# Sliding-window attention before a SwiGLU block: each query block scored on the 128 keys up to its end, and another opening order

## The chip, the cores and the metric

One core of a Trainium2 chip. The metric is the device time of one execution in microseconds (us). The span in a profile, from the first to the last instruction, is some 2 us less. Engines: PE is TensorE (its weight loads are listed apart), DVE is VectorE, ACT is ScalarE, POOL is GpSimd; SP issues the DMAs. The granted clock is the share of full speed at which PE may run; in these traces it is 1.0 or 0.5 ("halved"). To turn is to transpose.

## The reference

```
q, k, v: (8 batches, 8 heads, 576 tokens, 64), float32
scores = q k^T / 8, kept where 0 <= i - j < 64; softmax; times v
x = (4608 tokens, 512)                      # the heads side by side
out = (silu(x w_gate) * (x w_val)) w_out    # 512 -> 1536 -> 512
```

## The kernel before

Tokens run through in 36 groups g of 128 (two query blocks of 64), in bf16. A group needs scores on its own 128 keys, and its first 64 queries also need the group before. Since 576 is 9 blocks of 64, in every ninth block a sequence starts, and nothing before it counts. The feed-forward works on tiles t of 512 tokens with 12 steps m; `gv` makes the two hidden products (in the PSUM buffers `g_ps` and `v_ps`) and the tanh, `finish` the two DVE operations `sg` and `hT`, one step later.

```
def scores(g, hs=(0, 1)):                  # two half calls a group
    ...
    for h in hs:
        for i in range(2):
            for a in range(2):             # two row tiles of 64: 128 queries on own keys
                matmul(ps[a][:, i, 0:P], tokens(kT, g, p, a), tokens(qT, g, p, a), tile_position=(64 * a, 0))
            if prev:                       # 64 queries on the keys of the group before
                for a in range(2): matmul(ps[a][:, i, P:n], tokens(kT, g - 1, p, a), ...)
        for a in range(2):
            act.activation(e, ps[a][:, :, 0:n], AF.Exp, scale=0.125)
            dve.tensor_mul(e, e, mk...)    # the mask, 128x384
...
def cast_v(n, eng, cs=(0, 1)): ...         # one cast of 128x512 a group, on POOL
...
loads(0); loads(1); weights_gv(0..2)       # the opening
warm(30)                                   # dummy matmuls
pack(0, "k_f", dve); pack(0, "q_f", act); turn_k(0); turn_q(0)   # turned on PE in fp32
scores(0); scores(1); ... turn_x(3)        # groups 0 to 3
for m in range(12): step(0, m) ...         # only then feed-forward of tile 0
...
for w in range(8, NG):                     # the steady loop, one group a round
    step(t, 3 * s);     scores(w + 6, (0,)); turn_x(w + 4)
    step(t, 3 * s + 1); scores(w + 6, (1,)); products(w + 5, (0,))
    step(t, 3 * s + 2); products(w + 5, (1,)); ...; project(t - 1, s)
```

The softmax here doesn't subtract the row's maximum and nothing guards it: scores larger than these inputs give would overflow.

## Time and profile before

| | before |
|---|---|
| time | 389.8 us (2 runs, 389.55 to 390.04) |
| span | 387.1 us |
| PE busy | 361.2 us, 93% |
| mean granted clock of PE | 0.960 |
| loop with attention, 22 rounds | 203.3 us (122.1 to 325.4) |

Of the groups of instructions, these three are what the change replaces (busy us, mean ns of one, then idle time ahead of them and what ended it):

```profile
L171 DVE TENSOR_TENSOR E<-E,mask 128x384 bf16<-128x384 bf16 (+1 forms) x144 | 54.1, 383 | 73.5 <-ACT E L170 71.1
...
L170 ACT ACTIVATE E<-s_ps 128x384 bf16<-128x384 f32 (+1 forms) x144 | 61.1, 477 | 24.9 <-PE s_ps L164 21.6
...
L140 POOL CAST vb<-v_f 128x512 bf16<-128x512 f32 x36 | 23.3, 653 | 11.0 <-DMA v_f<-in_v_dram 10.3
```

An idle time counts only on an engine that is the bound, and these three are not. They matter as neighbours of PE.

### The profile page before, as it was taken

Reading aid. Unit: us, or ns where it says so; the run is one execution under the profiler, and the core shown is the slowest. Engines: PE = TensorE matmul, PEld = TensorE weight load, DVE = VectorE, ACT = ScalarE, POOL = GpSimd, SP = SyncE. Lnnn points to the kernel's source line nnn. Section 1 sums busy time; section 2 is a strip of 40 time slices with the busy share of each in tenths; the row PEclk is TensorE's granted clock in tenths of the full one; section 3 lists DMA queues with packets and bytes.
Section 4 is the critical chain, followed back from the end, with each engine's and each line's share of the span. In section 5 each row is a group of like instructions: output and inputs, shape, how many; then the busy total and the mean of one; then the engine's idle time right before and its main releaser. Section 6 shows DMA issues by size and latency. Waiting matters only on the chain.

```text
span 387.1 us, 7051 instructions
## 1 busy us (share of the span) xinstructions
PE 361.2 (93%) x2674; PEld 189.0 (49%) x2718; DVE 247.2 (64%) x552; ACT 185.8 (48%) x358; POOL 65.0 (17%) x82
## 2 busy tenths in 40 slices
PE   8679988988878999999999999999999999999996
PEld 3443455855555444444444444444444444444442
DVE  3764797856665666667666666766666667654430
ACT  2464769635456554444544444454444554332321
POOL 4403142502142103030302022020302000000000
PEclk9756999999996999999999999999999999999999
DMA  9969999719539587696967667686828000000102
GB/s 205 300 195 242 323 323 217 156 39 180 152 73 187 127 122 152 144 168 120 164 142 145 134 141 143 131 150 124 163 62 180 32 30 27 30 27 27 56 33 103
DMA packets 130849, 52.89 MB, mean 137 GB/s; under 512 B 102144, under 2 KB 124672, under 8 KB 130816
## 3 DMA queue, kind: packets, MB, share of 16 engines
q1 hardware_dynamic: 130816, 52.44, 62.2%
q8 instruction: 21, 0.34, 0.4%
q14 instruction: 12, 0.10, 0.1%
HBM read 37.75 MB, written 9.44 MB: 122 GB/s over the span
## 4 chain that ended last, share of the span: by engine, by line
PE 83%; ACT 5%; DMA 4%; DVE 4%; issue 1%; SPq 1%; POOL 0%; POOLq 0%; ACTq 0%
PE o_ps L263 24%; PE g_ps L246 21%; PE v_ps L246 21%; PE s_ps L158 4%; PE ao_ps L186 3%; DMA k_f<-in_k_dram 3%; PE xtp L210 3%; ACT E L170 2%; PE w_ps L275 2%; PE tp L116 2%; DVE E L171 2%; PE ao_ps L191 2%; DMA v_f<-in_v_dram 2%; DVE x_b L197 1%; PE s_ps L164 1%
## 5 line engine op out<-in xcount | busy, mean ns | idle before, releaser
L246 PE MATMUL g_ps<-xT,wg 128*128 128x512 bf16 (+1 forms) x458 | 113.5, 364 | 4.8 <-DVE sg L257 2.8
L246 PE MATMUL v_ps<-xT,wv 128*128 128x512 bf16 (+1 forms) x469 | 113.3, 362 | 0.6
L171 DVE TENSOR_TENSOR E<-E,mask 128x384 bf16<-128x384 bf16 (+1 forms) x144 | 54.1, 383 | 73.5 <-ACT E L170 71.1
L263 PE MATMUL o_ps<-wo,hT 128*128 128x512 bf16 x421 | 96.7, 379 | 0.5
L257 DVE SCALAR_TENSOR_TENSOR sg<-th,g_ps 128x512 f32<-128x512 f32 (+1 forms) x120 | 75.2, 627 | 24.4 <-ACT th L251 24.3
L251 ACT ACTIVATE th<-g_ps 128x512 f32<-128x512 f32 (+1 forms) x120 | 66.7, 556 | 48.9 <-PE g_ps L246 45.7
L258 DVE TENSOR_TENSOR hT<-sg,v_ps 128x512 bf16<-128x512 f32 (+1 forms) x120 | 76.1, 634 | 9.2 <-DVE sg L257 0.5
L170 ACT ACTIVATE E<-s_ps 128x384 bf16<-128x384 f32 (+1 forms) x144 | 61.1, 477 | 24.9 <-PE s_ps L164 21.6
L246 PEld LDWEIGHTS <-wv 128*128 128x128 bf16 x480 | 47.7, 99 | 49.0 <-issue 2.7
L246 PEld LDWEIGHTS <-wg 128*128 128x128 bf16 x480 | 44.4, 99 | 39.9 <-issue 6.8
L263 PEld LDWEIGHTS <-hT 128*128 128x128 bf16 x432 | 40.7, 98 | 44.7
L158 PE MATMUL s_ps<-qT,kT 64*128 64x128 bf16 x288 | 25.5, 225 | 11.2 <-ACT E L170 5.6
L123 POOL CAST q_fb<-q_f 128x1024 bf16<-128x1024 f32 x10 | 10.4, 1040 | 136.4 <-DMA q_f<-in_q_dram 120.4
L197 DVE TENSOR_TENSOR x_b<-ao_ps,r 128x256 bf16<-128x256 f32 x72 | 30.6, 425 | 2.5
L186 PE MATMUL ao_ps<-vb,E 128*128 128x65 bf16 x288 | 27.4, 201 | 2.1 <-DVE x_b L197 1.6
L158 PEld LDWEIGHTS <-kT 64*128 64x128 bf16 x288 | 14.1, 96 | 28.7 <-issue 26.0
L186 PEld LDWEIGHTS <-E 128*128 128x128 bf16 x288 | 21.7, 102 | 8.9 <-DVE x_b L197 2.2
L211 ACT COPY xT<-xtp 128x512 bf16<-128x512 bf16 x36 | 21.3, 591 | 8.4 <-PE xtp L210 8.4
L140 POOL CAST vb<-v_f 128x512 bf16<-128x512 f32 x36 | 23.3, 653 | 11.0 <-DMA v_f<-in_v_dram 10.3
L191 PE MATMUL ao_ps<-vb,E 128*128 128x65 bf16 x256 | 25.1, 201 | 0.0
L191 PEld LDWEIGHTS <-E 128*128 128x128 bf16 x256 | 19.3, 102 | 3.3
L109 POOL CAST k_fw<-k_f 128x1024 bf16<-128x1024 f32 x7 | 9.6, 1370 | 66.0 <-DMA k_f<-in_k_dram 29.0
(72 smaller groups left out, 181.2 us busy)
## 6 DMA issues: line engine op xcount, KB each, us to landing
v_f<-in_v_dram SPq DMA_DIRECT2D x32, 256.0 KB, 5.9
k_f<-in_k_dram SPq DMA_DIRECT2D x20, 256.0 KB, 3.9
q_f<-in_q_dram SPq DMA_DIRECT2D x20, 256.0 KB, 4.2
w_f<-in_moe_w_gate_dram SPq DMA_DIRECT2D x6, 512.0 KB, 6.6
w_f<-in_moe_w_val_dram SPq DMA_DIRECT2D x6, 512.0 KB, 6.7
wo_f<-in_moe_w_out_dram SPq DMA_DIRECT2D x6, 512.0 KB, 6.5
k_f<-in_k_dram SPq DMA_DIRECT2D x5, 512.0 KB, 6.1
q_f<-in_q_dram SPq DMA_DIRECT2D x5, 512.0 KB, 6.1
```

The costliest lines, as they stand in the source:

```text
L140: eng.tensor_copy(vb[n % VR][:, c, :, 0:D], v_f[:, c])
L158: nc.tensor.matmul(ps[a][:, i, 0:P], tokens(kT, g, p, a), tokens(qT, g, p, a), tile_position=(64 * a, 0),)
L170: act.activation(e, ps[a][:, :, 0:n], AF.Exp, scale=0.125)
L171: dve.tensor_mul(e, e, mk[:, 0:n].unsqueeze(1).to_broadcast([P, 2, n]))
L186: nc.tensor.matmul(o_ps[:, i, :], E[:, y, 0:P], vb[g // 2 % VR][:, g % 2, y, :], start=True, stop=not prev,)
L191: nc.tensor.matmul(o_ps[:, i, :], E[:, y, P:2 * P], vb[(g - 1) // 2 % VR][:, (g - 1) % 2, y, :], start=False, stop=True,)
L197: dve.tensor_mul(x_b[:, 256 * h:256 * h + 256].rearrange("r (y d) -> r y d", y=4), o_ps[:, :, 0:D], r[:].unsqueeze(2).to_broadcast([P, 4, D]),
L246: nc.tensor.matmul(ps[:, 0:n], w[:, c, P * m:P * m + P], xT[t][:, c, c0:c0 + n], start=(c == 0), stop=(c == 3),)
L251: act.activation(th[:, 0:n], g_ps[:, 0:n], AF.Tanh, scale=0.5)
L257: dve.scalar_tensor_tensor(sg[:, 0:n], th[:, 0:n], 1.0, g_ps[:, 0:n], ALU.add, ALU.mult)
L258: dve.tensor_mul(hT[t][:, m, c0:c0 + n], sg[:, 0:n], v_ps[:, 0:n])
L263: nc.tensor.matmul(o_ps[:], hT[t][:, c, P * s:P * s + P], wo[:, c, :], start=(c == 0), stop=(c == 11),)
```

## The change

A block of 64 queries needs just the 128 keys that end with it. So each block is scored on those: 16 matmuls of 64 columns a group instead of 8 of 128 and 8 of 64. For that the key ring holds 64 keys of overlap (`keys_before`), the values are kept at two offsets (`vo`, and `ve` shifted by 64), and scores are one call a group. k and q are turned on PE in bf16 for load blocks 0 to 3, of 256 tokens each (`turn2`; before: in fp32, for blocks 0 to 7) and by DMA after (`turn1`). POOL takes over casts of weights and triples those of values. The opening mixes half-tile steps and short runs of dummy matmuls into the first groups.

```
-    KR, VR, ER, QR = 3, 3, 3, 3
+    KR, VR, ER, QR = 3, 5, 3, 3
-    kT = [cst.tile([P, 4, 256], BF16, ...)]
+    kT = [cst.tile([P, 4, 320], BF16, ...)]
-    vb = [cst.tile([P, 2, H, VW], BF16, ...)]
+    vo = [cst.tile([P, H, VW], BF16, ...)];  ve = [cst.tile([P, H, VW], BF16, ...)]
+    def keys_before(n):
+        if n: dve.tensor_copy(kT[n % KR][:, :, 0:64], kT[(n - 1) % KR][:, :, 256:320])
+    def cast_v(g, eng, parts=(0, 1, 2)):     # vo, and the two halves of ve
+    ...
+    def scores(g):
+        for b in range(2):
+            for p in range(4):
+                for a in range(2):
+                    matmul(ps[a][:, p, 1 - b], kT[...][y, p, o:o + P], qT[...][y, p, o:o + 64], ...)
+        for a in range(2):
+            act.activation(e, ps[a][:], AF.Exp, scale=0.125)      # 128x512
+            dve.tensor_mul(e, e, mk...)
 ... opening, first part, then the loop
-    warm(30)
-    pack(0, "k_f", dve); pack(0, "q_f", act); cast_v(0, pool); turn_k(0); turn_q(0)
-    scores(0); scores(1); ... products(3); turn_x(2); turn_x(3); ... for m in range(12): step(0, m)
+    warm(16); KQ(0, "k_f", dve, dve); KQ(0, "q_f", act, act); cast_v(0, pool); cast_v(1, pool)
+    warm(2); scores(0); scores(1); warm(2); products(0); casts_gv(0); warm(2); products(1); turn_x(0)
+    cast_k(1, "k_f", pool); warm(2); turn_x(1); warm(2); cast_k(1, "q_f", pool); A(0, 0); ...
-            scores(w + 6, (0,))
+            scores(w + 6)
-            scores(w + 6, (1,))
```

More of the change, by code (lines that the diff above doesn't have):

```diff
@@ L52 @@
     wo = cst.tile([P, 12, DM], BF16, name="wo")
-    kT = [cst.tile([P, 4, 256], BF16, name=f"kT{i}") for i in range(KR)]
+    kT = [cst.tile([P, 4, 320], BF16, name=f"kT{i}") for i in range(KR)]
     qT = [cst.tile([P, 4, 256], BF16, name=f"qT{i}") for i in range(QR)]
-    vb = [cst.tile([P, 2, H, VW], BF16, name=f"vb{i}") for i in range(VR)]
-    Es = [cst.tile([P, H, 256], BF16, name=f"E{i}") for i in range(ER)]
-    masks = [cst.tile([P, P + 64], BF16, name=f"mask{i}") for i in range(2)]
-    ident = cst.tile([P, P], FP32, name="ident")
+    vo = [cst.tile([P, H, VW], BF16, name=f"vo{i}") for i in range(VR)]
+    ve = [cst.tile([P, H, VW], BF16, name=f"ve{i}") for i in range(VR)]
+    Es = [cst.tile([P, 25, 64], BF16, name=f"E{i}") for i in range(ER)]
+    masks = [cst.tile([P, 2, 64], BF16, name=f"mask{i}") for i in range(3)]
     identb = cst.tile([P, P], BF16, name="identb")
@@ L85, in load @@
             )
-        staged[nm, n] = x_f
+        staged[nm, n] = x_f[:].rearrange("r h c d -> r c h d")
     def load1(n, src, nm):
@@ L93, in load1 @@
                 sp.dma_start(x_f[r:r + m, i], src[b, :, s:s + t, :].rearrange("h r d -> r h d"))
-        staged[nm, n] = x_f
+        staged[nm, n] = x_f[:]
     def load_v(n):
@@ L99 @@
     words = {}
-    def pack(n, nm, eng):
-        x_f = staged.pop((nm, n))
-        x_w = cast.tile([P, H * D], FP32, name=nm + "w", tag=nm + "w")
-        y = x_w[:].bitcast(BF16).rearrange("r (h d c) -> r h c d", h=H, c=2)
-        if eng is act:
-            act.copy(y, x_f[:])
-        else:
-            eng.tensor_copy(y, x_f[:])
-        words[nm, n] = x_w
-    def turned(n, nm):
-        x_w = words.pop((nm, n))
-        tp = ps_a.tile([P, 4, P], FP32, name="tp", tag="a")
-        for p in range(4):
-            nc.tensor.transpose(tp[:, p, :], x_w[:, P * p:P * p + P], ident[:])
-        return tp[:].rearrange("r p x -> r (p x)").bitcast(BF16).rearrange(
-            "r (p x) -> r p x", p=4
-        )
@@ L121, in cast1, with copy, cast_k @@
-    def cast1(n, nm, eng):
+    def copy(eng, y, x):
+        if eng is act:
+            act.copy(y, x)
+        else:
+            eng.tensor_copy(y, x)
+    def cast_k(n, nm, eng):
+        x_f = staged.pop((nm, n))
         x_b = cast.tile([P, 2, DM], BF16, name=nm + "b", tag=nm + "b")
-        eng.tensor_copy(x_b[:], staged.pop((nm, n))[:].rearrange("r c h d -> r c (h d)"))
+        copy(eng, x_b[:].rearrange("r c (h d) -> r c h d", h=H), x_f)
         words[nm, n] = x_b
-    def turn1(n, nm, ring):
+    def keys_before(n):
+        if n:
+            dve.tensor_copy(kT[n % KR][:, :, 0:64], kT[(n - 1) % KR][:, :, 256:320])
@@ L127, in turn1 @@
+    def turn1(n, nm):
         x_b = words.pop((nm, n))
         for i in range(2):
-            sp.dma_start_transpose(out=ring[n % len(ring)][:, :, P * i:P * i + P], in_=x_b[:, i])
-    def turn_k(n, eng=None):
-        (eng or dve).tensor_copy(kT[n % KR][:], turned(n, "k_f"))
-    def turn_q(n):
-        act.copy(qT[n % QR][:], turned(n, "q_f"))
-    def cast_v(n, eng, cs=(0, 1)):
-        v_f = staged["v_f", n]
-        for c in cs:
-            eng.tensor_copy(vb[n % VR][:, c, :, 0:D], v_f[:, c])
@@ L142, in tokens @@
-    def tokens(ring, g, p, a, n=P):
-        o = P * (g % 2)
-        return ring[g // 2 % len(ring)][64 * a:64 * a + 64, p, o:o + n]
-    def scores(g, hs=(0, 1)):
-        E = Es[g % ER]
-        m = 2 * g
-        prev = m % 9 != 0
-        n = P + 64 if prev else P
-        mk = masks[1] if (m + 1) % 9 == 0 else masks[0]
-        for h in hs:
-            ps = [ps_a.tile([P, 2, P + 64], FP32, name="s_ps", tag="a") for _ in range(2)]
-            for i in range(2):
-                p = 2 * h + i
+            o = P * i + (64 if nm == "k_f" else 0)
@@ new lines, in turn1, with turn2 @@
+            ring = kT[n % KR] if nm == "k_f" else qT[n % QR]
+            sp.dma_start_transpose(out=ring[:, :, o:o + P], in_=x_b[:, i])
+    def turn2(n, nm, eng):
+        x_b = words.pop((nm, n))
+        tp = ps_a.tile([P, 4, 2, P], BF16, name="tp", tag="a")
+        for c in range(2):
+            for p in range(4):
+                nc.tensor.transpose(tp[:, p, c], x_b[:, c, P * p:P * p + P], identb[:])
+        o = 64 if nm == "k_f" else 0
+        ring = kT[n % KR] if nm == "k_f" else qT[n % QR]
+        y = ring[:, :, o:o + 256].rearrange("r p (x c) -> r p x c", c=2)
+        copy(eng, y, tp[:].rearrange("r p c x -> r p x c"))
@@ new lines, in cast_v @@
+    def cast_v(g, eng, parts=(0, 1, 2)):
+        x = staged["v_f", g // 2][:, g % 2]
+        lo, hi = slice(0, 64), slice(64, P)
+        for i in parts:
+            if i == 0:
+                copy(eng, vo[g % VR][:, :, 0:D], x)
+            if i == 1:
+                copy(eng, ve[g % VR][hi, :, 0:D], x[lo])
+            if i == 2 and g + 1 < NG:
+                copy(eng, ve[(g + 1) % VR][lo, :, 0:D], x[hi])
+    def scores(g):
+        E = Es[g % ER]
+        mk = masks[0]
+        for b in range(2):
+            if (2 * g + b) % 9 == 0:
+                mk = masks[2 - b]
+        ps = [ps_a.tile([P, 4, 2, 64], FP32, name="s_ps", tag="a") for _ in range(2)]
+        for b in range(2):
+            o = P * (g % 2) + 64 * b
+            for p in range(4):
@@ L157, in scores @@
                 for a in range(2):
+                    y = slice(64 * a, 64 * a + 64)
                     nc.tensor.matmul(
-                        ps[a][:, i, 0:P], tokens(kT, g, p, a), tokens(qT, g, p, a),
-                        tile_position=(64 * a, 0),
-                    )
-                if prev:
-                    for a in range(2):
-                        nc.tensor.matmul(
-                            ps[a][:, i, P:n], tokens(kT, g - 1, p, a), tokens(qT, g, p, a, 64),
-                            tile_position=(64 * a, 0),
-                        )
@@ L168, in scores @@
-            for a in range(2):
-                e = E[:, 4 * h + a:4 * h + 4:2, 0:n]
-                act.activation(e, ps[a][:, :, 0:n], AF.Exp, scale=0.125)
-                dve.tensor_mul(e, e, mk[:, 0:n].unsqueeze(1).to_broadcast([P, 2, n]))
+                        ps[a][:, p, 1 - b], kT[g // 2 % KR][y, p, o:o + P],
+                        qT[g // 2 % QR][y, p, o:o + 64], tile_position=(64 * a, 0),
+                    )
+        for a in range(2):
+            e = E[:, 1:25].rearrange("r (h y) x -> r h y x", y=3)[:, a:H:2, 0:2, :]
+            act.activation(e, ps[a][:], AF.Exp, scale=0.125)
+            dve.tensor_mul(e, e, mk[:].unsqueeze(1).to_broadcast([P, 4, 2, 64]))
@@ L179, in products @@
         x_b = xb[g]
-        E = Es[g % ER]
+        E = Es[g % ER][:].rearrange("r y x -> r (y x)")
         for h in hs:
@@ L184, in products @@
                 y = 4 * h + i
-                prev = 2 * g % 9 != 0
+                e = 192 * y
                 nc.tensor.matmul(
-                    o_ps[:, i, :], E[:, y, 0:P], vb[g // 2 % VR][:, g % 2, y, :],
-                    start=True, stop=not prev,
-                )
-                if prev:
-                    nc.tensor.matmul(
-                        o_ps[:, i, :], E[:, y, P:2 * P],
-                        vb[(g - 1) // 2 % VR][:, (g - 1) % 2, y, :], start=False, stop=True,
-                    )
+                    o_ps[:, i, :], E[:, e + P:e + 2 * P], ve[g % VR][:, y, :],
+                    start=True, stop=False,
+                )
+                nc.tensor.matmul(
+                    o_ps[:, i, :], E[:, e:e + P], vo[g % VR][:, y, :], start=False, stop=True,
+                )
             r = att.tile([P, 4], FP32, name="r", tag="r")
@@ L219, in weights_gv, with casts_gv @@
             raw[i, s] = w_f
-    def casts_gv(s):
-        dve.tensor_copy(wg[:, :, 256 * s:256 * s + 256], raw.pop((0, s))[:])
-        act.copy(wv[:, :, 256 * s:256 * s + 256], raw.pop((1, s))[:])
+    def casts_gv(s, eg=dve, ev=act):
+        copy(eg, wg[:, :, 256 * s:256 * s + 256], raw.pop((0, s))[:])
+        copy(ev, wv[:, :, 256 * s:256 * s + 256], raw.pop((1, s))[:])
     def weights_o(s):
@@ L230, in casts_o @@
     def casts_o(s, eng):
-        x = raw.pop((2, s))
-        if eng is act:
-            act.copy(wo[:, 2 * s:2 * s + 2, :], x[:])
-        else:
-            eng.tensor_copy(wo[:, 2 * s:2 * s + 2, :], x[:])
+        copy(eng, wo[:, 2 * s:2 * s + 2, :], raw.pop((2, s))[:])
     hT = {}
@@ L275, in warm @@
             nc.tensor.matmul(w_ps[:], wz[:, 0:P], wz[:])
-    def loads(n):
-        load(n, k, "k_f")
-        load(n, q, "q_f")
-        load_v(n)
-    loads(0)
-    loads(1)
-    for s in range(3):
-        weights_gv(s)
-    dve.memset(wz[:], 0.0)
-    make_identity(nc, ident[:])
-    for mk in masks:
-        dve.memset(mk[:], 1.0)
-    for E in Es:
-        pool.memset(E[:, :, 192:256], 0.0)
-    dve.tensor_copy(identb[:], ident[:])
-    for y, lo, hi in ((slice(0, P), 0, 63), (slice(P, P + 64), P, -65)):
-        w = y.stop - y.start
-        if lo == 0:
-            pool.affine_select(
-                out=masks[0][:, y], in_=masks[0][:, y], compare_op=ALU.is_ge, fill=0.0,
-                base=0, pattern=[[1, w]], channel_multiplier=-1,
-            )
-        pool.affine_select(
-            out=masks[0][:, y], in_=masks[0][:, y], compare_op=ALU.is_ge, fill=0.0,
-            base=hi, pattern=[[-1, w]], channel_multiplier=1,
-        )
-    dve.tensor_copy(masks[1][:], masks[0][:])
-    dve.memset(masks[1][0:64, 64:P], 0.0)
-    for x in vb:
-        dve.memset(x[:, :, :, D:VW], 1.0)
-    warm(30)
-    pack(0, "k_f", dve)
-    pack(0, "q_f", act)
-    cast_v(0, pool)
-    turn_k(0)
-    turn_q(0)
-    scores(0)
-    scores(1)
-    pack(1, "k_f", pool)
-    pack(1, "q_f", pool)
-    products(0)
-    turn_k(1)
-    products(1)
-    turn_x(0)
-    turn_q(1)
-    turn_x(1)
-    scores(2)
-    scores(3)
-    cast_v(1, pool)
-    casts_gv(0)
-    products(2)
-    products(3)
-    turn_x(2)
-    turn_x(3)
-    weights_gv(3)
-    loads(2)
     pend = None
@@ L344, in flush @@
         pend = None
-    for m in range(12):
-        if m % 2 == 0 and m // 2 + 1 < 6:
-            casts_gv(m // 2 + 1)
-        step(0, m)
-        if m == 1:
-            weights_gv(4)
-            weights_gv(5)
-        if m == 2:
-            loads(3)
-            pack(2, "k_f", pool)
-            pack(2, "q_f", pool)
-            cast_v(2, pool)
-        if m == 3:
-            for s in range(6):
-                weights_o(s)
-        if m == 4:
-            turn_k(2)
-        if m == 5:
-            turn_q(2)
-            pack(3, "k_f", pool)
-            pack(3, "q_f", pool)
-        if m == 6:
-            scores(4)
-        if m == 7:
-            products(4)
-            turn_k(3)
-        if m == 8:
-            scores(5)
-            turn_x(4)
-        if m == 9:
-            products(5)
-            turn_q(3)
-            loads(4)
-            cast_v(3, pool)
-        if m == 10:
-            turn_x(5)
-            scores(6)
-        if m == 11:
-            products(6)
-            for s in range(3):
-                casts_o(s, act)
@@ L386 @@
-    for m in range(12):
-        step(1, m, 0, 256)
-        if m == 0:
-            turn_x(6)
-            scores(7)
-        if m == 1:
-            products(7)
-            for s in range(3, 6):
-                casts_o(s, act)
-        if m == 2:
-            pack(4, "k_f", pool)
-            pack(4, "q_f", pool)
-            cast_v(4, pool)
-            turn_x(7)
-            loads(5)
-        if m == 5:
-            turn_k(4)
-        if m == 6:
-            turn_q(4)
-        if m == 9:
-            scores(8)
@@ L407 @@
-    flush()
-    project(0, 0)
-    for m in range(12):
-        step(1, m, 256, 256)
-        if m == 0:
-            pack(5, "k_f", pool)
-            pack(5, "q_f", pool)
-            cast_v(5, pool)
-            loads(6)
-            products(8)
-        if m == 2:
-            turn_x(8)
-            turn_k(5)
-            project(0, 1)
-        if m == 4:
-            scores(9)
-            turn_q(5)
-        if m == 6:
-            project(0, 2)
-            products(9)
-        if m == 7:
-            turn_x(9)
-            scores(10)
-        if m == 8:
-            products(10)
-            pack(6, "k_f", pool)
-            pack(6, "q_f", pool)
-            loads(7)
-        if m == 10:
-            turn_x(10)
-            scores(11)
-            turn_k(6)
@@ L439, with begin @@
-    flush()
-    project(0, 3)
+    def begin():
+        dve.memset(wz[:], 0.0)
+        make_identity(nc, identb[:])
+        for mk in masks:
+            dve.memset(mk[:], 1.0)
+        pool.affine_select(
+            out=masks[0][:], in_=masks[0][:], compare_op=ALU.is_ge, fill=0.0,
+            base=64, pattern=[[0, 2], [1, 64]], channel_multiplier=-1,
+        )
+        pool.affine_select(
+            out=masks[0][:], in_=masks[0][:], compare_op=ALU.is_ge, fill=0.0,
+            base=-1, pattern=[[0, 2], [-1, 64]], channel_multiplier=1,
+        )
+        dve.memset(kT[0][:, :, 0:64], 0.0)
+        dve.memset(ve[0][0:64], 0.0)
+        for x in vo + ve:
+            dve.memset(x[:, :, D:VW], 1.0)
+        for E in Es:
+            dve.memset(E[:, 0:25:3, :], 0.0)
+        for i in (1, 2):
+            dve.tensor_copy(masks[i][:], masks[0][:])
+            dve.memset(masks[i][0:64, i - 1, :], 0.0)
@@ new lines, in A, with B, F, KQ @@
+    def A(t, *ms):
+        for m in ms:
+            step(t, m, 0, 256)
+    def B(t, *ms):
+        for m in ms:
+            step(t, m, 256, 256)
+    def F(t, *ms):
+        for m in ms:
+            step(t, m)
+    def KQ(n, nm, eng, ev):
+        cast_k(n, nm, eng)
+        if nm == "k_f":
+            keys_before(n)
+        turn2(n, nm, ev)
+    load(0, k, "k_f")
+    load(0, q, "q_f")
+    load_v(0)
+    weights_gv(0)
+    load(1, k, "k_f")
+    load(1, q, "q_f")
+    weights_gv(1)
+    load_v(1)
@@ new lines @@
+    weights_gv(2)
+    begin()
+    warm(16)
+    KQ(0, "k_f", dve, dve)
+    KQ(0, "q_f", act, act)
+    cast_v(0, pool)
+    cast_v(1, pool)
+    warm(2)
+    scores(0)
+    scores(1)
+    warm(2)
+    products(0)
+    casts_gv(0)
+    warm(2)
+    products(1)
+    turn_x(0)
+    cast_k(1, "k_f", pool)
+    warm(2)
+    turn_x(1)
+    warm(2)
+    cast_k(1, "q_f", pool)
+    A(0, 0)
+    keys_before(1)
+    turn2(1, "k_f", dve)
+    A(0, 1)
+    warm(4)
+    turn2(1, "q_f", act)
+    load(2, k, "k_f")
@@ new lines @@
+    load(2, q, "q_f")
+    weights_gv(3)
+    load_v(2)
+    casts_gv(1)
+    warm(5)
+    scores(2)
+    warm(4)
+    A(0, 2)
+    scores(3)
+    cast_v(2, pool)
+    cast_v(3, pool)
+    A(0, 3)
+    products(2)
+    warm(3)
+    products(3)
+    warm(3)
+    turn_x(2)
+    casts_gv(2, pool)
+    turn_x(3)
+    weights_gv(4)
+    weights_gv(5)
+    A(0, 4)
+    cast_k(2, "k_f", pool)
+    B(0, 0)
+    keys_before(2)
+    B(0, 1)
+    turn2(2, "k_f", dve)
+    A(0, 5)
+    cast_k(2, "q_f", pool)
@@ new lines @@
+    B(0, 2)
+    B(0, 3)
+    turn2(2, "q_f", act)
+    B(0, 4)
+    casts_gv(3, pool)
+    B(0, 5)
+    load(3, k, "k_f")
+    load(3, q, "q_f")
+    load_v(3)
+    scores(4)
+    F(0, 6)
+    cast_v(4, pool)
+    cast_v(5, pool)
+    scores(5)
+    F(0, 7)
+    products(4)
+    casts_gv(4, pool)
+    for s in range(6):
+        weights_o(s)
+    F(0, 8)
+    products(5)
+    turn_x(4)
+    casts_gv(5, pool)
+    F(0, 9)
+    turn_x(5)
+    load1(4, k, "k_f")
+    load1(4, q, "q_f")
+    load_v(4)
@@ new lines @@
+    F(0, 10)
+    cast_k(3, "k_f", pool)
+    cast_k(3, "q_f", pool)
+    cast_v(6, pool)
+    cast_v(7, pool)
+    F(0, 11)
+    keys_before(3)
+    turn2(3, "k_f", dve)
+    A(1, 0)
+    turn2(3, "q_f", act)
+    A(1, 1)
+    for s in range(3):
+        casts_o(s, pool)
+    A(1, 2)
+    scores(6)
+    A(1, 3)
+    scores(7)
+    products(6)
+    for s in range(3, 6):
+        casts_o(s, pool)
+    A(1, 4)
+    turn_x(6)
+    products(7)
+    A(1, 5)
+    turn_x(7)
+    cast_k(4, "k_f", pool)
@@ new lines @@
+    cast_k(4, "q_f", pool)
+    turn1(4, "k_f")
+    turn1(4, "q_f")
+    keys_before(4)
+    load1(5, k, "k_f")
+    load1(5, q, "q_f")
+    load_v(5)
+    B(1, 0)
+    F(1, 6)
+    cast_v(8, pool)
+    cast_v(9, pool)
+    F(1, 7)
+    scores(8)
+    F(1, 8)
+    products(8)
+    F(1, 9)
+    turn_x(8)
+    scores(9)
+    cast_k(5, "k_f", pool)
+    cast_k(5, "q_f", pool)
+    turn1(5, "k_f")
+    turn1(5, "q_f")
+    keys_before(5)
+    load1(6, k, "k_f")
+    load1(6, q, "q_f")
+    load_v(6)
@@ L441 @@
+    F(1, 10)
+    products(9)
+    cast_v(10, pool)
+    cast_v(11, pool)
+    F(1, 11)
+    turn_x(9)
+    scores(10)
+    project(0, 0)
+    B(1, 1)
+    products(10)
+    B(1, 2)
+    cast_k(6, "k_f", pool)
+    cast_k(6, "q_f", pool)
+    turn1(6, "k_f")
+    turn1(6, "q_f")
+    keys_before(6)
+    load1(7, k, "k_f")
+    load1(7, q, "q_f")
+    load_v(7)
+    turn_x(10)
+    scores(11)
+    project(0, 1)
+    B(1, 3)
     products(11)
-    turn_q(6)
+    cast_v(12, pool)
+    B(1, 4)
+    turn_x(11)
@@ L443 @@
     scores(12)
-    turn_x(11)
-    pack(7, "k_f", pool)
-    pack(7, "q_f", pool)
+    project(0, 2)
+    B(1, 5)
+    products(12)
+    cast_v(13, pool)
+    cast_k(7, "k_f", pool)
+    turn1(7, "k_f")
+    keys_before(7)
+    cast_k(7, "q_f", pool)
+    turn1(7, "q_f")
     load1(8, k, "k_f")
     load1(8, q, "q_f")
-    cast_v(6, pool)
-    turn_k(7)
     scores(13)
-    products(12)
-    load_v(8)
-    cast_v(7, pool)
-    turn_q(7)
-    cast1(8, "k_f", pool)
-    turn1(8, "k_f", kT)
+    project(0, 3)
@@ L460 @@
+    cast_k(8, "k_f", pool)
+    turn1(8, "k_f")
+    keys_before(8)
     load1(9, k, "k_f")
@@ L469 @@
         if odd and n + 5 < NB:
-            cast1(n + 5, "k_f", pool)
+            cast_k(n + 5, "k_f", pool)
         if not odd and n + 4 < NB:
-            cast1(n + 4, "q_f", pool)
+            cast_k(n + 4, "q_f", pool)
         step(t, 3 * s + 1)
-        if w + 6 < NG:
-            scores(w + 6, (1,))
         if w + 5 < NG:
             products(w + 5, (0,))
-        if n + 4 < NB:
-            cast_v(n + 4, pool, (odd,))
+        if w + 6 < NG:
+            cast_v(w + 6, pool)
         step(t, 3 * s + 2)
@@ L483 @@
         if odd and n + 5 < NB:
-            turn1(n + 5, "k_f", kT)
+            turn1(n + 5, "k_f")
+            keys_before(n + 5)
         if not odd and n + 4 < NB:
-            turn1(n + 4, "q_f", qT)
+            turn1(n + 4, "q_f")
         project(t - 1, s)
@@ L489 @@
             load1(n + 5, q, "q_f")
-            load_v(n + 5)
+        if odd and n + 4 < NB:
+            load_v(n + 4)
         if not odd and n + 6 < NB:
```

## The prediction

> **What bounds the kernel now.** I read the page's second part first: the span in 40 slices of 9.7 us, busy share in tenths, and the TensorE clock granted.
>
> ```profile
> PE   8679988988878999999999999999999999999996
> ...
> PEclk9756999999996999999999999999999999999999
> DMA  9969999719539587696967667686828000000102
> ```
>
> From slice 13 on PE reads 9 everywhere and the clock is full; in the first 12 slices PE reads 6 to 9, the clock falls to 5, and the DMA engines are nearly full at first. So there are two stages, and I cut the span there with the busy times by stretch (span, then busy us and instruction count of PE, PE's weight load, DVE, ACT, POOL, then clock, DMA share, GB/s):
>
> ```profile
> 0.00:29.60 29.60, 21.66 (x174) 12.95 (x175) 16.71 (x46) 14.40 (x26) 7.98 (x18) 0.75 0.91 236
> 29.60:61.90 32.30, 29.46 (x213) 15.16 (x217) 23.84 (x48) 20.26 (x34) 8.85 (x8) 0.91 1.13 289
> 61.90:122.10 60.20, 50.77 (x489) 36.69 (x491) 42.21 (x111) 33.66 (x72) 17.38 (x18) 0.93 0.69 138
> 122.10:326.30 204.20, 202.46 (x1527) 97.93 (x1556) 138.65 (x309) 99.60 (x199) 30.81 (x39) 1.00 0.64 124
> 326.30:387.10 60.80, 56.88 (x279) 26.25 (x283) 25.78 (x40) 17.89 (x30) 0.00 (x0) 1.00 0.13 48
> ```
>
> **The opening** (0 to 122.1, before the steady loop) has PE busy 102 of 122 us at a reduced clock. Its first feed-forward matmul starts only at 29.61. **The loop with attention** (22 rounds, 122.1 to 326.3) is PE alone, 202.5 of 204.2 us: 9.24 us a round. **The last six rounds** have at most remnants of attention; a pure feed-forward round takes 7.77 us (36 matmuls of 512 columns at 0.216). Attention thus costs a round 1.47 us. I looked where, in the timeline of PE over one round (start, duration):
>
> ```profile
> 215.71 1.03 PE L246 MATMUL v_ps<-xT,wv 128*128 128x512 bf16 x4
> 216.67 0.23 PE L158 MATMUL s_ps<-qT,kT 64*128 64x128 bf16 x2
> 216.74 0.19 PE L164 MATMUL s_ps<-qT,kT 64*128 64x64 bf16 x2
> 216.77 0.22 PE L158 MATMUL s_ps<-qT,kT 64*128 64x128 bf16 x2
> 216.82 0.19 PE L164 MATMUL s_ps<-qT,kT 64*128 64x64 bf16 x2
> 216.95 0.40 PE L210 MATMUL xtp<-identb,x_b 128*128 128x128 bf16 x4
> 217.18 1.03 PE L246 MATMUL g_ps<-xT,wg 128*128 128x512 bf16 x4
> ```
>
> Starts count here, since durations overlap. The four v matmuls should occupy 0.86 us, but the scores come 0.96 after them: 0.10 is lost entering. A pair with 128 columns takes 0.06 to 0.07, one with 64 columns 0.03; after the last pair 0.13 pass to the transpose, 0.10 of them lost. A half call of scores is 0.37 us, two in a round 0.74; the transpose of x takes 0.23, the two products 0.26 and 0.24. The sum is 1.47, as needed.
>
> **What the Trainium skill says.** "TensorE: Matmul & The Clock Gate", section "Back-to-back issue gap", gives N/2.4 GHz plus 2.5 ns start to start, and a floor near 25 ns at small N: the trace has 216 ns at 512 and about 28 at 64, so it agrees. "TensorEngine Tiling (Array Packing)", section "Key Properties", says that changing the tiling mode drains TensorE: the two losses of 0.10 around each scores call fit it. "SBUF — State Buffer", section "Who interferes with whom", says that a DVE instruction with two SBUF inputs contends with a GpSimd instruction that reads SBUF. The trace agrees: the mask multiply (E and mask both in SBUF) takes 0.36 us alone, but four of them right after this POOL cast began took 1.92:
>
> ```profile
> 119.37 1.92 DVE L171 TENSOR_TENSOR E<-E,mask 128x384 bf16<-128x384 bf16 x4 [0.26 <-ACT E L170]
> ...
> 119.23 1.04 POOL L123 CAST k_fb<-k_f 128x1024 bf16<-128x1024 f32 x1 [8.27 <-DMA k_f<-in_k_dram]
> ```
>
> The clock page's summary table ("Why this matters for your kernels") warns of PE idle gaps over about 3 us; in the opening the clock was halved over 20 us from about 14.6 on, so that too is seen.
>
> **The change, part by part: the loop.** Scores are now one call a round: 0.096 in, eight pairs of 64 columns at 0.028 (0.224), about 0.01 start, 0.097 out: 0.43 us against 0.74. Minus 0.31. Pairs keep that pace only if the weight loads do; before, a 64-column pair is followed by the next after 28 ns with its loads started just with it, so I think so. Products stay at 16 matmuls (blocks on sequence boundaries lose their saving: two rounds, together about +0.6 us). Exp becomes 2 of 128x512 instead of 4 of 128x384: from 381 ns at 256 columns and 489 at 384, about 0.6 each. Masks: 0.29 at 256 and 0.36 at 384 give 0.42 at 512, two for four.
>
> The new burst is a catch. DVE runs in order, and the feed-forward's sg of step 3s is behind both masks; sg frees the g bank that step 3s+2 writes. Counting from the round's first matmul: scores in PSUM at 2.22, exps end 2.85 and 3.35, second mask starts 3.38, sg 3.72 to 4.40, bank free about 4.46. PE wants it at 2.16 (scores out) + 0.23 + 1.73 (step 3s+1) + 0.26 (first product) = 4.38. So about 0.08 a round is given back (before: sg ended at 4.05, wanted at 4.68). Net: 9.24 - 0.31 + 0.08 = about 9.0; 22 rounds save 5.3, less 0.6: 4.7 us.
>
> POOL: three value casts a block (0.617 each) instead of one. Per two rounds it goes from 3.3 us of casts to 2 x 1.04 + 6 x 0.6 = 5.8, in one burst when q lands. In the trace that burst starts 5.7 to 7.0 us into an even round; ending 5.6 later, it ends 2.4 to 3.7 us into the odd round, just where the masks stand (2.9 to 3.8). When it collides, masks and sg slip by 0.5 to 1 us and PE waits that long. I take 2 us for some of the 11 odd rounds. The key-overlap copy adds about 0.2 us of DVE every second round, hidden: DVE has 30% idle. Loop: minus 3 us.
>
> **The change: the opening.** Same feed-forward work: 24 steps x 1.73 = 41.5, four projections x 2.59 = 10.4. Attention of 14 groups: scores 14 x 0.43 = 6, products 13 x 0.5 = 6.5, x transposes 2.8. Transposes of k and q: 16 turns of four fp32 ones (0.44) become 8 of eight bf16 ones (0.45), minus 3.4; the rest go by DMA. Dummy matmuls: 30 become 45 (16 + 29 spread out): 9.7. PE at full clock: 80.5 us. The loads up to there, 25 MB in the first 125 us, need about 85 us at the 289 GB/s of the second stretch. So neither forces more than 85, while 122 was taken.
>
> What is gained is the start. Before, k and q of block 0 were cast at 5 to 8 us, but 30 dummy matmuls held PE until 9.4; then groups 0 to 3 ran as a latency chain with no feed-forward beside it until 29.6. Now 16 dummies end near 6.4; k's copy out ends near 8, q's near 10, scores near 10, products(0) near 13, and after two x transposes half-tile steps (256 tokens) start at about 17 to 18, and groups 2 and 3 run between them. I follow loads (w0 about 12, k and q of block 1 about 14 to 16, w1 19, v1 21, w2 24 us at 300 GB/s): A steps 0 to 3 done by about 28, groups 2 and 3 by 30; remaining feed-forward of tile 0 is 17.3 us plus groups 4 and 5 (4 us): tile 0 done about 52, before 61.9. Tile 1 with projections 31.2, groups 6 to 13 and the turns 9.2: 40 us, plus 4 to 8 us of waits (in-order queues, three PSUM buffers, masks behind POOL). Opening ends at 97 to 101; I take 100, minus 22 us.
>
> **Sum.** Span 387.1 - 22 - 3 = 362; the time is 2.7 above the span: about 365 us.
>
> **Rivals.** First: *POOL becomes the opening's bound.* It now casts w slices 2 to 5, all w_out, all k and q but the first, and triples values: about 55 us of the first 100. For: the mask multiplies are blocked by its reads (shown above). Against: half the time is still idle. It would make the opening 108 to 115, time 375 to 380. Second: *the burst in the loop turns into a wait of PE on sg in every round*, 0.3 to 0.5 us: the loop gains nothing, time near 369; with frequent POOL collisions 373. Third: *the halved clock persists*: the dummies at half clock cost double, tile 0 slips by 5 to 8 us, time 371. Fourth: *loads are the wall and the new order starves nothing*: opening near 92, time 357. Fifth: *everything gained in the opening is only waiting moved*, since DMA is nearly full in the first 60 us; then time 380. Against: the first feed-forward step needs only 4 MB, some 14 us.
>
> **Range and chances.** The opening spans 91 to 112 (time 356 to 377), the loop plus 2 to minus 7; together 354 to 378 for 8 in 10. The 2% line is 382.0; it takes the second rival and a bad first one together to pass it. Faster 0.91, same 0.07, slower 0.02.
>
> **What would show it.** First feed-forward matmul at 16 to 20 us instead of 29.6; loop beginning near 100; scores of a round in one run of eight pairs, about 0.43 us from v's end to the transpose; rounds near 9.0 us, with a small wait of g_ps for sg; some masks over 0.8 us beside POOL casts in odd rounds; last six rounds unchanged at 60.8. It is wrong if the loop starts after 112 (look at POOL and the clock), if even rounds are above 9.2 (weight loads too slow, or sg), or if the loads of weights are what the tile 0 steps wait for.

## The result, and the profile after

| | before | after |
|---|---|---|
| time | 389.8 us | 372.69 us (2 runs, 372.14 and 373.23) |
| span | 387.1 us | 370.2 us |
| PE busy | 361.2 us | 345.2 us |
| POOL busy | 65.0 us | 113.5 us |
| mean granted clock | 0.960 | 0.989 |

The ratio is 0.9561 (95% interval 0.9496 to 0.9626). Ratios here are the mean time of one kernel's fast runs over that of the other's of the same rounds, so not quite the ratio of the medians quoted. 372.69 lies in the stated range; the centre, 365, was 7.7 us too low.

The slices of the page after, of 9.3 us each:

```profile
PE   8787998989779999999999999999999999999995
...
POOL 2554585463314350605060606060605120000000
PEclk9999999999899999999999999999999999999999
```

The clock holds through the start; one dip stands in slice 11, where PE reads 7 twice. The trace has it from 95.6 to 99.0 us, and a second from 109.2 to 112.6, split between two slices. POOL is busy in every second slice of the loop. The groups that answer to those shown of before:

```profile
L168 DVE TENSOR_TENSOR E<-E,mask 128x512 bf16<-128x512 bf16 x72 | 36.9, 526 | 74.8 <-ACT E L167 73.4
...
L167 ACT ACTIVATE E<-s_ps 128x512 bf16<-128x512 f32 x72 | 39.1, 596 | 20.1 <-PE s_ps L161 20.1
L105 POOL CAST ve<-v_f 64x512 bf16<-64x512 f32 x71 | 44.3, 624 | 4.4
...
L105 POOL CAST vo<-v_f 128x512 bf16<-128x512 f32 x36 | 22.3, 621 | 25.8 <-DMA v_f<-in_v_dram 14.2
```

ACT and DVE save 22 and 17 us, off the critical path. A mask takes 526 ns on average where an undisturbed one of this size takes 426 ns: something delays some of them. A cast of 64 partitions costs as much as one of 128.

The busy times by stretch, cut at the first feed-forward matmul, the end of tile 0, and the first and last of the 22 rounds (columns as in the prediction):

```profile
0.00:16.80 16.80, 12.72 (x113) 6.29 (x115) 9.77 (x39) 7.68 (x10) 7.69 (x16) 1.00 1.00 257
16.80:53.30 36.50, 32.34 (x335) 21.70 (x340) 28.12 (x63) 20.64 (x37) 20.28 (x28) 1.00 1.04 274
53.30:104.30 51.00, 44.20 (x467) 27.39 (x472) 36.37 (x86) 22.20 (x44) 25.22 (x32) 0.97 0.96 198
104.30:308.30 204.00, 198.06 (x1556) 99.41 (x1584) 131.00 (x276) 84.94 (x154) 60.36 (x85) 0.99 0.67 136
308.30:370.20 61.90, 57.91 (x284) 26.69 (x288) 25.84 (x41) 18.48 (x31) 0.00 (x0) 0.99 0.13 47
```

The feed-forward starts at 16.8 instead of 29.6, tile 0 ends at 53.3 instead of 61.4 (and tile 1 begins at 53.7 instead of 61.9), and the loop starts at 104.35 instead of 122.12. But the 22 rounds take 204.1 us, 0.8 more than the 203.3 of before, and PE is idle in 6 us of them. (The prediction's last cut, 326.3, lies 0.9 us after the end of the loop of before, so its 204.2 is that much too long and its 60.8 too short.) To see where the gain went I took the start of the output projection in each round, from the trace:

| | before | after |
|---|---|---|
| projection of the first round starts | 129.42 | 114.42, 15.0 earlier |
| from there, 21 rounds to that of the last | 193.41 (9.21 a round) | 191.44 (9.12 a round), 2.0 less |
| from there to the end of the span | 64.2 | 64.3 |

All of the 16.9 us are accounted for. Of the 17.8 us by which the loop starts earlier, 2.8 are lost in the loop's first round, which takes 10.1 us up to its projection instead of 7.3. The list of PE's waits between 53.3 and 108.5 us (us in total, times, longest) names the longest wait:

```profile
PE s_ps L161 <- DMA qT<-q_fb: 4.6, 2, 2.6
PE g_ps L237 <- DVE sg L248: 1.1, 2, 0.6
```

PE waits for a q turned by DMA, at 92.2 and 106.2; each of the two dips of the clock begins about 1 us after such a wait ends. The DMA queue in that stage (start and length of the issues, two to a line):

```profile
62.54 2.72 SPq L123 DMA_TRANSPOSE kT<-k_fb  x2
65.35 3.36 SPq L123 DMA_TRANSPOSE qT<-q_fb  x2
68.76 1.20 SPq L93 DMA_DIRECT2D k_f<-in_k_dram  x2
70.01 1.78 SPq L93 DMA_DIRECT2D q_f<-in_q_dram  x2
71.83 2.25 SPq L93 DMA_DIRECT2D v_f<-in_v_dram  x2
```

The issues follow each other almost without a gap: added up from the trace, they fill 47.3 of the stage's 51.0 us (in before, 26.4 of 60.2). The next turn of k stands at 74.60: one block of 256 tokens takes 12 us of this queue here, and the next two 15 and 13 (turns of k at 89.51 and 102.83). The stage takes 51.0 us for four blocks of scores, 12.8 a block.

In the loop, this is an odd round of the trace (all engines; start, length):

```profile
172.81 1.03 PE L237 MATMUL v_ps<-xT,wv 128*128 128x512 bf16 x4
173.77 0.41 PE L161 MATMUL s_ps<-qT,kT 64*128 64x64 bf16 x16
174.11 0.40 PE L205 MATMUL xtp<-identb,x_b 128*128 128x128 bf16 x4
...
174.79 1.36 POOL L105 CAST ve<-v_f 64x512 bf16<-64x512 f32 x2
174.84 1.59 DVE L168 TENSOR_TENSOR E<-E,mask 128x512 bf16<-128x512 bf16 x2 [2.98 <-ACT E L167]
...
176.35 0.67 DVE L248 SCALAR_TENSOR_TENSOR sg<-th,g_ps 128x512 f32<-128x512 f32 x1
177.08 1.02 PE L237 MATMUL g_ps<-xT,wg 128*128 128x512 bf16 x4 [0.60 <-DVE sg L248]
```

The first three lines are the one call of scores. Two masks that should take 0.9 us together take 1.59 behind two POOL casts, sg starts at 176.35, and PE stands for 0.60 until sg frees its bank.

### The profile page after: what moved, and what is told of

Read it like the earlier page. It is cut to its first block, busy times and chain, and to the rows that moved or that the text cites. A ratio compares the mean times of both kernels' runs of the same rounds, so it can differ in the third digit from the quotient of the medians.

```text
span 370.2 us, 7165 instructions
## 1 busy us (share of the span) xinstructions
PE 345.2 (93%) x2750; PEld 181.5 (49%) x2797; DVE 231.1 (62%) x503; ACT 154.0 (42%) x276; POOL 113.5 (31%) x159
## 4 chain that ended last, share of the span: by engine, by line
PE 74%; DVE 6%; DMA 6%; SPq 5%; ACT 5%; issue 2%; POOL 2%; ACTq 0%; POOLq 0%
PE o_ps L254 24%; PE g_ps L237 21%; PE v_ps L237 19%; DMA q_f<-in_q_dram 4%; SPq L93 4%; DVE E L168 3%; PE s_ps L161 3%; PE w_ps L266 2%; ACT E L167 2%; PE xtp L205 2%; PE ao_ps L183 2%; PE ao_ps L187 2%; DMA qT<-q_fb 1%; DVE sg L248 1%; SPq L123 1%
## 5 line engine op out<-in xcount | busy, mean ns | idle before, releaser
L254 PE MATMUL o_ps<-wo,hT 128*128 128x512 bf16 x419 | 98.4, 384 | 0.7
L168 DVE TENSOR_TENSOR E<-E,mask 128x512 bf16<-128x512 bf16 x72 | 36.9, 526 | 74.8 <-ACT E L167 73.4
L105 POOL CAST q_fb<-q_f 128x1024 bf16<-128x1024 f32 x17 | 17.9, 1053 | 114.6 <-DMA q_f<-in_q_dram 112.4
L167 ACT ACTIVATE E<-s_ps 128x512 bf16<-128x512 f32 x72 | 39.1, 596 | 20.1 <-PE s_ps L161 20.1
L105 POOL CAST ve<-v_f 64x512 bf16<-64x512 f32 x71 | 44.3, 624 | 4.4
L105 POOL CAST vo<-v_f 128x512 bf16<-128x512 f32 x36 | 22.3, 621 | 25.8 <-DMA v_f<-in_v_dram 14.2
L105 POOL CAST k_fb<-k_f 128x1024 bf16<-128x1024 f32 x17 | 18.1, 1063 | 38.1 <-DMA k_f<-in_k_dram 32.6
L183 PE MATMUL ao_ps<-ve,E 128*128 128x65 bf16 x288 | 26.6, 194 | 2.2 <-DVE x_b L192 1.2
L187 PE MATMUL ao_ps<-vo,E 128*128 128x65 bf16 x288 | 26.6, 194 | 0.0
L161 PE MATMUL s_ps<-qT,kT 64*128 64x64 bf16 x576 | 14.9, 191 | 7.3 <-DMA qT<-q_fb 4.6
```

The source lines that it names most:

```text
L105: eng.tensor_copy(y, x)
L161: nc.tensor.matmul(ps[a][:, p, 1 - b], kT[g // 2 % KR][y, p, o:o + P], qT[g // 2 % QR][y, p, o:o + 64], tile_position=(64 * a, 0),)
L167: act.activation(e, ps[a][:], AF.Exp, scale=0.125)
L168: dve.tensor_mul(e, e, mk[:].unsqueeze(1).to_broadcast([P, 4, 2, 64]))
L183: nc.tensor.matmul(o_ps[:, i, :], E[:, e + P:e + 2 * P], ve[g % VR][:, y, :], start=True, stop=False,)
L187: nc.tensor.matmul(o_ps[:, i, :], E[:, e:e + P], vo[g % VR][:, y, :], start=False, stop=True,)
```

## The experiments

Eight kernels on one chip, each with runs of the kernel before; all gave correct results. Before took 388.86 and 388.89 us. The kernel after was timed in other rounds on its own; against it I compare ratios to before (0.9561) and stages of the traces.

**1. Loads first.** The loads of blocks 5 to 8 are moved ahead of the casts and turns of the block before them.

```
+    load1(5, k, "k_f"); load1(5, q, "q_f"); load_v(5)
     cast_k(4, "k_f", pool); cast_k(4, "q_f", pool)
     turn1(4, "k_f"); turn1(4, "q_f"); keys_before(4)
-    load1(5, k, "k_f"); load1(5, q, "q_f"); load_v(5)
     ... the same for 6, 7 and 8
```

> Changed kernel with the loads of blocks 5 to 8 issued ahead of the casts and turns of the block before, nothing else moved. Theory (queue order): in tile 1 of the opening PE waits 4.6 us on the turned q, because each block's loads stand in the DMA queue behind the turns of the block before, which wait on POOL casts; one block takes 13 us round that ring. Then both waits for qT go and the steady loop begins 4 to 7 us earlier: 366 to 368.5 us against 372.7. Rival (DMA bandwidth or POOL sets the pace of the blocks): the waits only move, at least 371.5 us.

384.44 us, ratio 0.9888 (0.9859 to 0.9917). The queue-order theory missed; the rival's bound of 371.5 holds, but it did not expect a loss of this size. PE now waits 12.3 us for qT, three times, and the first round's projection starts at 126.96. The trace shows how: the 6 us of loads now stand ahead of the turns in the same queue, so that the first turn of tile 1 starts at 68.1 instead of 62.5, PE falls behind, and then the queue waits 5.4 us at a store of the first projection before it reaches the load of block 7 (issued at 93.2). The waits of PE, and of the queue between 85 and 95 us:

```profile
PE s_ps L161 <- DMA qT<-q_fb: 12.3, 3, 4.6
...
SPq L261 <- ACT th L242: 5.4, 1, 5.4
```

So it was not the fault that the loads stood behind the turns. That the queue has too much issue time in it, so that each thing put ahead delays the rest, was the reading of this trace which experiment 5 then tests.

**2. Masks late.** In the loop, the mask multiplies are emitted behind the next step, so that DVE does sg and hT of step 3s first. Their products come a round later in any case.

```
-            scores(w + 6)
+            scores(w + 6, late=True)        # without the multiplies
         step(t, 3 * s + 1)
+            mask(w + 6)
```

> Changed kernel with the mask multiplies of the steady loop put behind the next step's sg and hT, so that DVE does not hold the g bank behind a mask that waits for a POOL cast. Theory (mask ahead of sg): no wait of g_ps for sg in the loop, rounds 8.93 to 8.97 us instead of 9.12, odd and even rounds alike although masks beside POOL casts still take over 0.8 us; 22 rounds save 3.5 to 4 us: 368.5 to 369.5. Rival (the rounds are long because short score pairs wait for their weight loads, or from the drain): rounds stay at 9.1, at least 371.5 us.

368.36 us, ratio 0.9470 (0.9438 to 0.9502). Every round is 8.92 us, odd and even alike, and PE's list of waits in the loop is empty. The collisions are still there, as in this odd round on DVE, where the two masks take 1.02 us beside POOL casts:

```profile
243.73 0.69 DVE L256 SCALAR_TENSOR_TENSOR sg<-th,g_ps 128x512 f32<-128x512 f32 x1 [2.12 <-ACT th L250]
244.53 0.69 DVE L257 TENSOR_TENSOR hT<-sg,v_ps 128x512 bf16<-128x512 f32 x1
245.13 1.02 DVE L176 TENSOR_TENSOR E<-E,mask 128x512 bf16<-128x512 bf16 x2
```

sg is ahead of them, so they cost nothing. This settles the loop: short score pairs are not slow. The changed kernel's rounds without a collision are 9.01, so 0.09 a round is the mask standing ahead of sg even undisturbed, and 9.12 on average less 9.01 is what the collisions add.

**3. Both edits.**

> Both edits, loads first and masks late. If the two causes are separate their gains add: 362 to 365 us. If one gain is given back by the other (the loop starts earlier, but POOL and loads then fall at other times), 366 or more.

380.59 us, ratio 0.9795 (0.9762 to 0.9828). The rounds are again 8.92, the opening is as late as in experiment 1 (127.12). The two effects add, as they should, but the first has the wrong sign.

**4. The opening of before, with everything else new.** Its order of loads, casts and stages, with the new functions in place of the old (`cast_k` for `pack`, `turn2` for `turn_k` and `turn_q`, two value casts for one).

```
-    warm(16); KQ(0, "k_f", dve, dve); ... project(0, 3); cast_k(8, "k_f", pool); ...
+    loads(0); loads(1); weights_gv(0..2); begin(); warm(30)
+    cast_k(0, "k_f", dve); cast_k(0, "q_f", act); cast_v(0, pool); cast_v(1, pool)
+    keys_before(0); turn2(0, "k_f", dve); turn2(0, "q_f", act); scores(0); scores(1); ...
```

> The new scoring, values in two alignments and the new loop, but the opening of before: its order of loads, casts and stages, 30 dummy matmuls at the start and none later, k and q of blocks 0 to 7 turned on PE in the new bf16 way. Theory (most of the gain is the opening's order): 382 to 388 us, the loop still 9.1 us a round, first feed-forward matmul near 28 us. Rival (the scoring is the gain, the order only moved waits): 373 to 378 us.

380.86 us, ratio 0.9803 (0.9775 to 0.9830), a little below what the theory expected. The first feed-forward matmul is at 28.8, the clock is halved for 17 us (before: 20), rounds take 9.11. The first round's projection starts at 123.50: between before (129.42) and after (114.42). So up to there 5.9 us come from the new functions (scores, turns, casts of values) and 9.1 from the rest; with 2.0 from the loop these are the 17. That rest is not the order alone: the half-tile steps, the later dummies, the turns of blocks 4 to 7 by DMA and the casts of weights on POOL came with it, and this run doesn't tell them apart.

**5. Blocks 4 to 7 turned on PE.** Built on experiment 2: k and q of these blocks are loaded in token pairs, which halves their DMAs, and turned by PE, which takes the turns out of the queue.

```
-    load1(5, k, "k_f"); load1(5, q, "q_f")
+    load(5, k, "k_f"); load(5, q, "q_f")
-    turn1(5, "k_f"); turn1(5, "q_f"); keys_before(5)
+    keys_before(5); turn2(5, "k_f", dve); turn2(5, "q_f", act)     # ahead of F(1, 11)
     ... the same for 4, 6 and 7
```

> The masks-late kernel, with k and q of blocks 4 to 7 loaded in token pairs and turned on PE (as blocks 0 to 3 are), not by DMA. The loads-first run fell: PE waited 12.3 us for turned q, more than before. New theory: in tile 1 the one DMA queue is itself full, its issues follow each other without a gap from 44 to 112 us, and a block needs 12 to 14 us of it, of which the turns are 5 to 6 and the k and q loads half as long in pairs. Then with no turns in it the waits for qT (5.4 us) go and PE pays 8 x 0.45 = 3.6 us of transposes: 364 to 368 us against 368.4, the opening's queue with gaps in it. Rival (POOL's casts pace the blocks, whoever turns them): the waits reappear on tp for a cast, 369 us or more.

364.35 us, ratio 0.9366 (0.9338 to 0.9393): the fastest kernel, 4.0 us below experiment 2 although PE does more. No wait for qT is left; PE waits 1.0 us once for a POOL cast. The first round's projection starts at 111.85 (114.52 in experiment 2), and in the profiled run the clock is never halved. The queue now has gaps:

```profile
73.73 4.01 SPq L93 DMA_DIRECT2D v_f<-in_v_dram  x3
87.71 0.38 SPq L269 DMA_DIRECT2D out_dram<-os__1530  x1
```

Between 77.7 and 87.7 nothing is issued. This supports the queue as what delayed q, and speaks against POOL, whose casts stay as they were. Turns and half of the k and q issues left the queue together, so their shares are not told apart. A rival stays open: the DMA engines themselves. From experiment 2 to this one, between the start of tile 1 and the loop, the issues fell from 48.4 of 53.1 us to 31.1 of 51.3, but the DMA share fell too, from 0.89 to 0.83; and since the issue of one and the same kind of load took from 0.6 to 2.1 us in this stage of the kernel after, the two may hang together. And the stage still takes 51.3 us, now with eight turns on PE; it is the first round that became short, 6.3 us up to its projection instead of 7.8.

**6. Loads from the ACT queue.** Built on experiment 2: the loads of blocks 5 to 8 in the opening are issued by ACT.

```
-    load1(5, k, "k_f"); load1(5, q, "q_f"); load_v(5)
+    load1(5, k, "k_f", act); load1(5, q, "q_f", act); load1(5, v, "v_f", act)
     ... the same for 6, 7 and 8
```

> The masks-late kernel, with the loads of blocks 5 to 8 in the opening issued from the ACT queue, the turns and stores left where they are. Theory (the one queue is full of issue time): half of a block's queue time goes to ACT, which is 45% busy, the waits for qT go and the loop begins 4 to 6 us earlier: 363 to 365 us. Rival (the 16 DMA engines or POOL are the limit): loads land no sooner, waits for qT stay at 4 us or more, 367 us or more. A third possibility: ACT, in order, is held by its issues and PE waits for th or exp, slower than 369.

381.87 us, ratio 0.9820 (0.9796 to 0.9843): the third possibility. ACT's own trace:

```profile
86.51 2.26 ACTq L93 DMA_DIRECT2D q_f<-in_q_dram  x3
88.86 2.24 ACTq L93 DMA_DIRECT2D v_f<-in_v_dram  x3
91.23 1.09 ACT L250 ACTIVATE th<-g_ps 128x512 f32<-128x512 f32 x2 [5.49 <-DMA q_f<-in_q_dram]
```

What stands behind the issues in ACT's order waits for them: ACT is idle for 5.5 us before th (7.2 in another place, 8.4 before a copy of xT), and PE waits for sg (8.5 us in all, up to 5.3 at once) and for exp (4.9). One wait for qT, of 3.3 us, is left. Whether another idle queue would help is open; the test only shows that ACT is not one.

**7. No dummies after the first 16.**

```
-    warm(2) ... warm(3)      # all ten later calls, 29 matmuls
```

> The changed kernel without the 29 dummy matmuls after the first 16. Theory (they hold the granted clock): the clock is halved again somewhere between 10 and 35 us as in the kernel before, tile 0 ends 3 to 6 us later, 375 to 379 us. Rival (they fill gaps or stand in the way): the clock stays full or the loss is hidden behind loads, 370 to 373.5 us.

373.41 us, ratio 0.9598 (0.9569 to 0.9628) against 0.9561. The clock is halved from 12.6 to 19.4 and from 29.7 to 33.1 us, as the theory said, but tile 0 ends only 0.6 us later, and the time is as the rival said. The loop even begins a little earlier (103.6 instead of 104.35). Its first projection starts 2.0 us later (116.37) because of the turned q again, with a wait of 3.5 us there and a halved clock from 108.2 to 115.0. Rounds of 9.09 give some of it back, and the time is 0.7 us higher, a ratio inside the interval of the kernel after (0.9496 to 0.9626). The dummies hold the clock through the start, but a gain from that is not shown. That PE waits for others in these stretches would explain it; this was not tested.

**8. Before, with 16 dummies instead of 30.**

```
-    warm(30)
+    warm(16)
```

> The kernel before with 16 dummy matmuls at the start instead of 30. My prediction said that the 30 held PE until 9.4 us while k was cast at 5.7. If that delay counts, the first groups and the first feed-forward step come 2 to 3 us earlier and the time falls to 386 to 388 us. Rival (loads of weights or the halved clock set the opening): within 0.5 us of before, or slower because the clock is halved sooner.

387.84 us, ratio 0.9975 (0.9950 to 1.0000): about 1 us, and 2 at most. The time lies in the range that was given for the delay, but what was to bring it about did not happen: k is turned at 6.1 instead of 9.3, yet the first feed-forward matmul comes at 28.7, only 0.9 earlier. The clock is halved sooner, from 11.0 us on instead of 14.6, and PE waits 1.6 us for q's cast on ACT. An early start alone is thus worth little. That the half-tile steps between the groups bring the feed-forward forward is argued: no run has them alone.

## Why the prediction was right

**Scores on PE.** Predicted 0.43 us a call; measured 0.436 from v's end to the transpose of x (0.096 in, pairs 29 ns apart, 0.126 from the last pair to the transpose). The round with nothing in its way was to be 9.24 - 0.31 = 8.93; experiment 2 has 8.92.

**sg behind the masks.** Predicted 0.08 a round; 9.01 less 8.92 is 0.09. **POOL collisions** in odd rounds were put at 2 us in all; 9.12 less 9.01, times 22, is some 2.3. The second was a guess from where the burst ends, and that it came out so near is partly luck; experiment 2 shows that both are one mechanism, DVE's order. The loop was to save 3 us and saves 2.0. Half of this miss is a sum: 0.23 a round over 22 rounds is 5.1, not 5.3, and with the other parts it makes 2.5, not 3.

**The start.** First feed-forward matmul at 16 to 20: 16.8. Tile 0 done at about 52: 53.3. But I gave as a reason that the 30 dummies held PE, and experiment 8 shows this to be worth about 1 us, so the right time came in part for a wrong reason. "The halved clock" was a rival worth 371; in experiment 7, where the clock is halved for 10 of the first 35 us, the time is 0.7 higher, within the noise.

**The term that was mis-sized** is the last of the opening: "Tile 1 with projections 31.2, groups 6 to 13 and the turns 9.2: 40 us, plus 4 to 8 us of waits (in-order queues, three PSUM buffers, masks behind POOL)". From the end of tile 0 to the loop it took 51.0 us, and the first round lost 2.8 more of the lead. In these 51.0 us the trace lists 6.1 of waits of PE, within the 4 to 8, but 2.6 of them are for the turned q; the dip that follows costs 1.7 more (an estimate, half of its 3.4 us), and about 3 us are left over for small gaps. In the first round stand the other 2.0 us for q and the other dip. I counted PE's work and the bytes of the loads, but not the issue time of the one DMA queue, although the change moves four blocks from turns on PE to turns by DMA into just that stage. "The rest go by DMA" was written as a saving. Its price is the 4.6 us of waits for qT and the two dips of the clock behind them; experiment 5 undoes it and gains 4.0, with the turns back on PE. Whether the issue time of the queue or the load of the DMA engines kept q back stays open. Of the named rivals, none was this one; against POOL as the bound speaks experiment 5. With 53.3 + 51.0 + 2.8 = 107 in place of 100, and 2 in place of 3 for the loop, the sum is 373, which is what was measured. (Its last step adds 2.7 us from span to time, but that pairs two different runs: the profiled one took 388.8, 1.7 more than its span.) What remains of tile 1's length in experiment 5 was not followed up.

## What to carry to other kernels

When work moves to DMA, count the issue time of the queue, and the load of the DMA engines, as you count an engine's: so many issues of such a length per block, against the time that the bound engine takes for a block. On an engine in order, put the operation that frees a buffer for the bound engine ahead of one that nobody awaits yet; here this made collisions with another engine harmless without removing one. And an expected saving by a transfer is to be checked in the stage where the transfers already stand close.

## What the Trainium skill lacked or had wrong

- "TensorE: Matmul & The Clock Gate", section "Back-to-back issue gap", says that a stream of weight loads and matmuls sustains about 81 ns at N=128 and 131 ns at N=512. Here such streams run at 56 and 216 ns, the formula that the page calls isolated; at 64 and 65 columns, with a new weight load each, at 29 to 30 ns.
- "TensorEngine Tiling (Array Packing)", section "Key Properties", states that a mode switch drains TensorE, with no size. Here entering the two-row mode costs 0.096 us and leaving it 0.097, in before and after, whether four or eight pairs lie between.
- "DMA: Bandwidth & Descriptors", section "Rules for kernel authors", says that spreading DMAs over engines only saves the sequencer's issue time. The section gives no such time, and the page has none measured for loads and turns like these. Here SP spent 47.3 of a stage's 51.0 us on issues: about 0.6 us for a load of 256 KB in 256-byte rows, 1.2 to 1.3 us for a turn of 128x512, often more (one load of q took 3.4). And on ACT it is taken from compute: 5.5 to 8.4 us without an activation for six to nine loads (experiment 6).
- "SBUF — State Buffer", section "Who interferes with whom", is right that a two-input DVE instruction is blocked by a POOL read; the size here: a mask of 0.43 us took up to 1.25.
- On "TensorE: Matmul & The Clock Gate", section "Why this matters for your kernels": keeping the clock up is not always worth its matmuls; 29 dummies kept it full through the start, and without them the time was 0.7 us higher, within the noise (experiment 7). The table there warns of idle gaps of PE over about 3 us. Here the clock of before was halved at 14.6 us although no gap until then was over 1.3 us, and that of after was halved behind waits of 2.6 and 2.0 us.
